# A new table of priority weights for the list scheduler of a top-k attention followed by two squared-ReLU feed-forward layers, one core

## The chip, the core and the metric

One core of a Trainium2 chip runs the whole program. Its engines work side by side, each through its own list of instructions in the order written: TensorE (PE, with its weight loads PEld), VectorE (DVE), ScalarE (ACT), GpSimd (POOL), and SyncE (SP), which here issues the DMAs. The metric is device microseconds of one execution; times are given as the median of the runs.

## What is computed

The reference, cut to its core (4 batches, 8 heads, 576 positions, head size 64, so 2304 tokens of 512; the hidden layers have 2048 columns):

```python
scores = scale * q @ k.T
kth = np.partition(scores, -32, axis=-1)[..., -32:-31]
scores = np.where(scores >= kth, scores, -1e9)          # keep the 32 largest of each row
attn = softmax(scores); x = (attn @ v), heads side by side
x = (s * relu(x @ w_in)**2 + b) @ w_out                 # first layer
x = relu(x @ w2_in)**2 @ w2_out                         # second layer
```

## The kernel before, in words

**Tiles.** 18 tiles of 128 queries (tiles 4 and 13 are made of two half tiles of two batches), 8 heads each: 144 heads of work. A head is: scores on PE (`pS`, L606, four matmuls), four rounds of MAX8 and three of MATCH_REPLACE on DVE to find the 32nd largest value (L617, L628), the exponential on ACT (`et`, L631), the mask on DVE (L659 or L665, which is the last reader of `pS`), a copy to two fp16 parts `pn` on ACT (L661, L668) and POOL (L463), a DMA transpose `pT` (L682), and 15 matmuls with the values on PE (`pA`, L692). Two score buffers `pS0` and `pS1` are used in turn, so the scores of a head wait for the mask of the head two before it.

**Two layers.** After its 8 heads a tile is scaled and split into fp16 parts: ACT squares it and sums (L704), DVE and POOL make a power of two of the sum, ACT scales (L708) and rounds (L710), POOL takes the rest (L711), and a DMA transpose makes `xT` (L713). A layer then runs over one tile or two ("a unit") in chunks of 256 hidden values: an IN group on PE (`pH`, L784, 12 matmuls of 256 columns or 24 of 128), on ACT `rr` (L792, ReLU, the only reader of `pH`), `gh` (L794, the square in fp16) and `gg` or `sqr` (L797, the square in fp32), on POOL `gl` (L802, the rest of the square), and an OUT group on PE (`pC`, L828, 6 matmuls of 512 columns). There are 288 chunks in all. `pH` is one buffer, `rr` two, `gh` and `gl` three.

**Weights.** The four weight matrices arrive as 64-bit words, are made to floats on DVE, ACT and POOL, scaled and split into fp16 parts (ACT L955, L956 and others), between the first heads.

**What sets the order.** Every operation is added to a `Plan` with an engine, a duration of its own, and a priority. `Plan.order` plays the program through with these durations and takes on each engine, at each moment, the ready operation of the lowest priority number; the resulting order is emitted as it is and not changed afterwards. To the priority it adds two numbers of a table `TW`: one under the name of the kind of work (the "tag", such as `A2.1` for tile 2, heads 2 and 3, `F08` for unit 8 of the first layer, `X2` for the split of tile 2), and one under the name of the step (such as `ac18` for `rr`).

Of the kernel before, what the change touches and what calls it, by code (L numbers as in the profile page):

```python
# [9 lines left out]
F16 = mybir.dt.float16  # L10
# [63 lines left out]


TW = {
# [41 lines left out]
}  # L118

WAIT = {("dve", "dve"): 0.2, ("act", "act"): 0.2, ("pool", "pool"): 0.1, ("pe", "pe"): 0.0, ("sp", "sp"): 0.0,  # L120
# [1073 lines left out]
```

## Time and profile before

| | |
|---|---|
| three runs | 1146.24, 1151.6 (median), 1153.46 us |
| the profiled execution | 1145.25 us, of which the span from the first to the last instruction is 1143.5 us |
| PE | 1014.8 us busy (89%) |
| DVE | 941.7 us (82%) |
| ACT | 844.6 us (74%) |
| POOL | 676.8 us (59%) |
| mean granted clock of PE | 0.964 |

A busy time is the time in which an engine has at least one instruction running. A share over the whole span is a mean over stretches that are limited by different things, so the rows below are cut by stretch. "Idle before <- X" is the time an engine sat idle just ahead of an instruction, and what ended it.

### The profile page before, as it was taken

What the parts mean: (1) busy time and instruction counts of PE and PEld (TensorE: products, weight loads), DVE (VectorE), ACT (ScalarE), POOL (GpSimd) and SP (SyncE); (2) the same over time, 40 slices, a digit from 0 to 9 for tenths busy, and PEclk for the clock granted to TensorE, in tenths of its full rate; (3) what the DMA queues carried; (4) which work ended last, traced back from release to release, by engine and by line L of the source; (5) the groups of instructions that cost most, each with busy time, mean ns of one, the idle gap of its engine ahead of it and who ended that gap; (6) DMA issues with size and microseconds to landing.
All of it is one profiled execution on the core that took longest, in us unless ns stands there. A gap on an engine that the chain in (4) does not pass through costs nothing. (4 is left out here: it accounts for less than half of the span.)

```text
span 1143.5 us, 27272 instructions
## 1 busy us (share of the span) xinstructions
PE 1014.8 (89%) x10004; PEld 690.7 (60%) x10004; DVE 941.7 (82%) x2038; ACT 844.6 (74%) x2010; POOL 676.8 (59%) x1005
## 2 busy tenths in 40 slices
PE   1256768777899999999999999999999999999998
PEld 1133335465667667667766776666666665666765
DVE  6999999899989999999999999997999999400000
ACT  2368987689788777889987889778876776565554
POOL 5267867889667655665865568456654464342322
PEclk9978889778999999999999999999999999999999
DMA  9988966584966776389486655776385257214530
GB/s 268 335 213 230 238 145 174 174 174 80 204 160 130 139 170 128 94 187 197 95 183 148 128 113 128 171 148 124 98 183 124 58 114 180 61 29 144 170 120 29
DMA packets 338215, 171.13 MB, mean 150 GB/s; under 512 B 292513, under 2 KB 317089, under 8 KB 338081
## 3 DMA queue, kind: packets, MB, share of 16 engines
q1 hardware_dynamic: 338080, 169.39, 63.0%
q8 instruction: 78, 1.28, 0.5%
q14 instruction: 57, 0.46, 0.1%
HBM read 89.65 MB, written 8.91 MB: 86 GB/s over the span
## 5 line engine op out<-in xcount | busy, mean ns | idle before, releaser
L784 PE MATMUL pH<-xT,w 128*128 128x128 f16 (+1 forms) x4800 | 431.6, 244 | 11.5 <-ACT rr L792 10.9
L784 PEld LDWEIGHTS <-w 128*128 128x128 f16 x4800 | 362.5, 98 | 75.4 <-issue 15.6
L463 POOL TENSOR_TENSOR pn<-et,pn 128x576 f16<-128x576 f32 x144 | 186.8, 1299 | 84.5 <-ACT pn L668 31.3
L792 ACT ACTIVATE rr<-pH,rsc 128x256 f32<-128x256 f32 x288 | 134.6, 467 | 96.6 <-PE pH L784 95.5
L802 POOL TENSOR_TENSOR gl<-gg,gh 128x256 f16<-128x256 f32 x152 | 102.9, 677 | 119.2 <-ACT gh L794 89.6
L828 PE MATMUL pC<-wo,gh 128*128 128x512 f16 x576 | 172.8, 382 | 0.0
L828 PE MATMUL pC<-wring,gh 128*128 128x512 f16 x544 | 161.9, 379 | 1.3 <-DMA wring<-wo 1.2
L617 DVE MAX8 m<-spare 128x8 f32<-128x576 f32 x216 | 161.8, 749 | 1.2
L617 DVE MAX8 m<-wk 128x8 f32<-128x576 f32 x216 | 161.5, 748 | 0.9
L828 PEld LDWEIGHTS <-gh 128*128 128x128 f16 x1152 | 103.4, 98 | 76.0 <-issue 3.0
L802 POOL TENSOR_TENSOR gl<-sqr,gh 128x256 f16<-128x256 f32 x136 | 91.3, 671 | 96.1 <-ACT gh L794 71.9
L631 ACT ACTIVATE et<-pS,ngm,cq 128x576 f32<-128x576 f32 x144 | 118.7, 826 | 27.4 <-DVE spare L628 11.2
L794 ACT ACTIVATE gh<-rr 128x256 f16<-128x256 f32 x288 | 118.3, 411 | 10.8 <-PE pC L828 4.3
L617 DVE MAX8 m<-pS 128x8 f32<-128x576 f32 x144 | 108.3, 754 | 12.2 <-PE pS L606 11.7
L692 PE MATMUL pA<-vp,pT 128*128 128x64 f16 (+1 forms) x2400 | 95.7, 197 | 17.5 <-DMA pT<-pn 17.3
L692 PEld LDWEIGHTS <-pT 128*128 128x128 f16 (+1 forms) x2400 | 86.9, 103 | 39.8 <-DMA pT<-pn 24.5
L828 PE MATMUL pC<-wo,gl 128*128 128x512 f16 x288 | 109.8, 381 | 0.0
L606 PE MATMUL pS<-kT,qT 128*128 128x512 f16 (+2 forms) x320 | 85.5, 298 | 24.1 <-DVE et L659 14.6
L628 DVE MATCH_REPLACE8 wk<-m,wk 128x576 f32<-128x576 f32 x144 | 106.8, 741 | 0.0
L628 DVE MATCH_REPLACE8 spare<-m,spare 128x576 f32<-128x576 f32 x144 | 106.7, 741 | 0.0
L828 PE MATMUL pC<-wring,gl 128*128 128x512 f16 x272 | 103.2, 379 | 0.6 <-POOL gl L802 0.6
L828 PEld LDWEIGHTS <-gl 128*128 128x128 f16 x576 | 56.4, 98 | 70.9 <-POOL gl L802 3.1
(197 smaller groups left out, 1627.8 us busy)
## 6 DMA issues: line engine op xcount, KB each, us to landing
wring<-wo SPq DMA_DIRECT2D x72, 512.0 KB, 3.8
w<-in_moe_w_out_dram SPq DMA_DIRECT2D x16, 512.0 KB, 5.0
wring<-in_moe_w_in_dram SPq DMA_DIRECT2D x12, 512.0 KB, 4.7
xT<-in_moe_w_in_dram SPq DMA_DIRECT2D x12, 512.0 KB, 5.3
qW<-qT SPq DMA_DIRECT2D x36, 128.0 KB, 2.7
kvraw<-in_k_dram SPq DMA_DIRECT2D x16, 256.0 KB, 3.4
kvraw<-in_v_dram SPq DMA_DIRECT2D x16, 256.0 KB, 3.1
w<-in_moe_w_in_dram SPq DMA_DIRECT2D x8, 512.0 KB, 7.8
```

Source lines behind the costliest of these rows:

```text
L463: add(pool, step, c_pool(cols * (c.stop - c.start) / n), prio, lambda c=c: nc.gpsimd.tensor_tensor(o[:, c], x[:, c], y[:, c], op=op), r=r, ...
L606: nc.tensor.matmul(s[r0:r0 + n, c0:c0 + cn_], lhsT=w[:, h, r0:r0 + n], rhs=kk[:, k0:k0 + cn_], start=(a == 0), stop=(a == 1))
L617: add(dve, "dv10", 0.67, prio, lambda src=src, rd=rd: nc.vector.max(m[:, 8 * rd:8 * rd + 8], src), r=[sn], w=[f"m{i2}_{rd}"])
L628: add(dve, "dv11", 0.66, prio, lambda src=src, rd=rd: nc.vector.match_replace(wk, m[:, 8 * rd:8 * rd + 8], src, NEG), r=[sn, f"m{i2}_{rd}" ...
L631: add(act, "ac9", 0.72, prio, lambda: nc.scalar.activation(out=e, in_=s, func=ACTF.Exp, bias=ngm[i2][:, 0:1], scale=cq[q2][:, j:j + 1]), r ...
L692: nc.tensor.matmul(pA[r0:r0 + n, h, :], lhsT=pT[p3][:, a * 5 + c, r0:r0 + n], rhs=vv[:, vc, z, :], start=(c == 0 and a == 0 and z == 0), s ...
L784: nc.tensor.matmul(ps_, lhsT=win[:, ff, a, kk, :], rhs=x[:, z * KD + kk, :], start=(kk == 0 and a == 0 and z == 0), stop=(kk == KD - 1 and ...
L792: add(act, "ac18", 0.14 + n / 1200.0, prio, lambda r=r, rs=rs: nc.scalar.activation(out=r, in_=pH[:, 0:n], func=ACTF.Relu, scale=rs), r=[" ...
L794: add(act, "ac19", 0.094 + n / 1200.0, prio, lambda r=r, hi=hi: nc.scalar.activation(out=hi, in_=r, func=ACTF.Square), r=rrn, w=ghn)
L802: add(pool, "po19", 0.12 + n * 0.0021, prio, lambda gt=gt, hi=hi, lo=lo: nc.gpsimd.tensor_tensor(lo, gt, hi, op=ALU.subtract), r=[*gn, *gh ...
L828: nc.tensor.matmul(pC[tt], lhsT=src[g3][:, c], rhs=wt(a, ff), start=(ff == 0 and a == 0 and src is gh), stop=(ff == KF - 1 and src is gl))
```

## The change

Only the numbers of the table `TW` are different; all of its lines are. Two of them, before and after:

```diff
-    "A0.0": 9.3, "A0.1": -14.6, "A0.2": 61.0, "A0.3": -2.7, "A1.0": -26.5, "A1.1": 51.0, "A1.2": -52.3, "A1.3": -7.5,
...
-    "sp7": -38.5, "sp8": -29.8, "sp9": -14.1, "store": 31.5,
+    "A0.0": -6.7, "A0.1": -39.6, "A0.2": 49.4, "A0.3": -5.2, "A1.0": -36.3, "A1.1": 48.0, "A1.2": -41.9, "A1.3": 22.4,
...
+    "sp8": 35.9, "sp9": 64.5, "store": 2.4,
```

No operation is added, removed or altered. The same instructions stand on the same engines, in an order that differs in many small places. Three of them follow.

**First place, ACT, while the last weights of the second layer are split and tile 3 is attended.** `xs0_91` and `xn0_93` hold tile 2, `w2_68` the weights, `pn0` and `et` are of the heads; the last row is `rr` of the second layer's second chunk. Before:

```order
L704 ACTIVATE junk_89,xss2_200<-xs0_91 128x512
L523 ACTIVATE kvraw1_87<-kvraw1_87,ksc_138 128x576
L851 ACTIVATE xs1_92<-pC0_189,usc1_151 128x512
L661 ACTIVATE pn0_102,sums1_128<-et0_100 128x576
L525 CAST vp5_85<-kvraw1_87 128x9x64
L708 ACTIVATE xs0_91<-xs0_91,xsc2_144 128x512
L624 ACTIVATE ngm1_126<-m8_1_122,ncq1_134 128x1
L710 CAST xn0_93<-xs0_91 128x512
L631 ACTIVATE et1_101<-pS1_186,ngm1_126,cq1_132 128x576
L955 ACTIVATE w2_68<-w2_68,wsc2_172 128x512 x2
L956 CAST w2_68<-w2_68 128x512 x2
L792 ACTIVATE rr0_111<-pH_188,rsc1_182 128x256
```

In the change, from the `et1_101` row on, on the same engine:

```order
L631 ACTIVATE et1_101<-pS1_186,ngm1_126,cq1_132 128x576
L523 ACTIVATE kvraw1_87<-kvraw1_87,ksc_138 128x576
L593 ACTIVATE ncq0_133<-cq0_131 128x1
L525 CAST vp5_85<-kvraw1_87 128x9x64
L955 ACTIVATE w2_68<-w2_68,wsc2_172 128x512 x2
L956 CAST w2_68<-w2_68 128x512 x2
L792 ACTIVATE rr0_111<-pH_188,rsc1_182 128x256
```

The three rows on tile 2 (L704, L708, L710) and the copy of `pn0` (L661) no longer stand ahead of this `rr`. The three rows now come four and five chunks later:

```order
L704 ACTIVATE junk_89,xss2_200<-xs0_91 128x512
L704 ACTIVATE junk_89,xss5_203<-xs1_92 128x512
L792 ACTIVATE rr0_111<-pH_188,rsc1_182 128x256
L624 ACTIVATE ngm0_125<-m8_0_121,ncq1_134 128x1
L797 ACTIVATE gg_113<-rr0_111 128x256
L661 ACTIVATE pn1_103,sums1_128<-et1_101 128x576
L631 ACTIVATE et0_100<-pS0_185,ngm0_125,cq1_132 128x576
L794 ACTIVATE gh2_116<-rr0_111 128x256
L708 ACTIVATE xs0_91<-xs0_91,xsc2_144 128x512
L624 ACTIVATE ngm1_126<-m8_1_122,ncq1_134 128x1
L710 CAST xn0_93<-xs0_91 128x512
L792 ACTIVATE rr1_112<-pH_188,rsc1_182 128x256
```

The rows of DVE, POOL and SP on tile 2 (L449, L451, L453, L711, L713) move back with them.

**Second place, PE, just after that chunk: what follows the scores of a head.** `pS1` is the score buffer, `pA` the product with the values, `pH` an IN group. Before:

```order
L606 LDWEIGHTS qT1_96
L606 MATMUL pS1_186<-kT2_76,qT1_96 128x64
L606 LDWEIGHTS qW1_98
L606 MATMUL pS1_186<-kT2_76,qW1_98 128x64
L692 LDWEIGHTS pT2_106
L692 MATMUL pA_187<-vp1_81,pT2_106 128x64
```

In the change:

```order
L606 LDWEIGHTS qT1_96
L606 MATMUL pS1_186<-kT2_76,qT1_96 128x64
L606 LDWEIGHTS qW1_98
L606 MATMUL pS1_186<-kT2_76,qW1_98 128x64
L784 LDWEIGHTS w2_68
L784 MATMUL pH_188<-xT2_109,w2_68 128x128
```

The `pA` group has gone behind two IN groups and an OUT group.

**Third place, ACT in the last stretch, the second layer of the last units.** Each chunk has its three rows. Before:

```order
L792 ACTIVATE rr0_111<-pH_188,rsc1_182 128x256
L797 ACTIVATE gg_113<-rr0_111 128x256
L794 ACTIVATE gh1_115<-rr0_111 128x256
L792 ACTIVATE rr1_112<-pH_188,rsc1_182 128x256
L797 ACTIVATE sqr_90<-rr1_112 128x256
L794 ACTIVATE gh2_116<-rr1_112 128x256
```

In the change:

```order
L792 ACTIVATE rr0_111<-pH_188,rsc1_182 128x256
L794 ACTIVATE gh1_115<-rr0_111 128x256
L797 ACTIVATE gg_113<-rr0_111 128x256
L792 ACTIVATE rr1_112<-pH_188,rsc1_182 128x256
L794 ACTIVATE gh2_116<-rr1_112 128x256
L797 ACTIVATE sqr_90<-rr1_112 128x256
```

`gh` now comes ahead of `gg`. On PE the same stretch reads IN, OUT, IN, OUT in both, but an OUT group belongs to the third IN group before it in the kernel before, and to the second in the change (at the very end four OUT groups follow the last IN group before, three in the change).

## Rows read from the trace of the kernel before

**Rows 1.** Busy time by stretch: us, each engine (instructions), PE clock, DMA share, GB/s.

```profile
0.00:300.00 300.00, 188.54 (x1650) 118.82 (x1651) 280.22 (x605) 216.47 (x469) 208.75 (x253) 0.86 0.78 202
300.00:985.00 685.00, 671.68 (x7090) 466.15 (x7087) 657.34 (x1421) 543.71 (x1346) 418.43 (x667) 1.00 0.65 140
985.00:1143.50 158.50, 154.61 (x1270) 105.75 (x1268) 4.17 (x14) 84.45 (x196) 49.61 (x86) 1.00 0.30 91
```

**Rows 2.** Chain of waits late in the span: start, us, an IN group, an OUT group.

```profile
1012.74 1.31 PE pH L784 x12
1014.05 1.29 PE pC L828 x6
```

**Rows 3.** Waits of PE from 300 us on: total us, times, longest.

```profile
PE pH L784 <- ACT rr L792: 4.4, 9, 0.9
PE pA L692 <- DMA pT<-pn: 3.5, 10, 0.7
PE pS L606 <- DVE et L665: 2.3, 4, 0.7
...
PE pC L828 <- POOL gl L802: 0.6, 2, 0.4
```

**Rows 4.** Busy time by stretch of 10 us, columns as in rows 1.

```profile
270.00:280.00 10.00, 3.19 (x38) 2.03 (x38) 10.00 (x27) 10.00 (x22) 9.82 (x20) 0.72 0.31 69
280.00:290.00 10.00, 8.68 (x104) 7.29 (x104) 8.80 (x18) 8.90 (x23) 9.31 (x10) 0.76 0.52 118
290.00:300.00 10.00, 8.55 (x124) 6.58 (x122) 9.75 (x21) 9.81 (x27) 7.60 (x13) 1.00 0.90 193
```

**Rows 5.** PE in order of time, 262 to 318 us: start, us, [idle before].

```profile
274.64 0.59 PE L606 MATMUL pS<-kT,qT 128*128 128x512 f16 x1 [2.74 <-DVE xsa L449]
...
278.12 0.98 PE L692 MATMUL pA<-vp,pT 128*128 128x64 f16 x15 [2.36 <-DMA pT<-pn]
280.70 2.72 PE L784 MATMUL pH<-xT,w 128*128 128x128 f16 x24 [1.60 <-ACT rr L792]
...
301.95 1.50 PE L784 MATMUL pH<-xT,w 128*128 128x128 f16 x24
```

**Rows 6.** ACT in order of time, 262 to 300 us: start, us.

```profile
272.80 0.62 ACT L704 ACTIVATE junk<-xs 128x512 bf16<-128x512 f32 x1
...
274.65 0.67 ACT L661 ACTIVATE pn<-et 128x576 f16<-128x576 f32 x1
...
275.88 0.72 ACT L708 ACTIVATE xs<-xs,xsc 128x512 f32<-128x512 f32 x1
...
276.68 0.61 ACT L710 CAST xn<-xs 128x512 f16<-128x512 f32 x1
...
280.17 0.47 ACT L792 ACTIVATE rr<-pH,rsc 128x256 f32<-128x256 f32 x1
```

**Rows 7.** DMA queue in order of time, 270 to 305 us: start, us of issue.

```profile
280.95 1.23 SPq L713 DMA_TRANSPOSE xT<-xn  x1
...
294.75 2.89 SPq L682 DMA_TRANSPOSE pT<-pn  x2
```

**Rows 8.** Issue to landing of these transposes, 270 to 310 us: min, median, max.

```profile
DMA to landing us min/median/max: 2.7/3.1/3.6
```

**Rows 9.** POOL in order of time, 275 to 303 us.

```profile
279.77 1.16 POOL L711 TENSOR_TENSOR xn<-xs,xn 128x512 f16<-128x512 f32 x1
...
296.68 0.19 POOL L867 TENSOR_TENSOR usc<-xsc,fc 128x1 f32<-128x1 f32 x1
```

**Rows 10.** DVE in order of time, 764 to 800 us.

```profile
776.41 0.15 DVE L449 TENSOR_SCALAR qsa<-qsc 128x1 int32<-128x1 int32 x1 [6.09 <-ACT junk L553]
...
778.86 0.77 DVE L617 MAX8 m<-pS 128x8 f32<-128x576 f32 x1 [2.11 <-PE pS L606]
```

**Rows 11.** ACT in order of time, 1000 to 1012 us.

```profile
1001.07 0.47 ACT L792 ACTIVATE rr<-pH,rsc 128x256 f32<-128x256 f32 x1 [1.11 <-PE pH L784]
```

**Rows 12.** POOL in order of time, 1000 to 1012 us.

```profile
1002.69 0.67 POOL L802 TENSOR_TENSOR gl<-gg,gh 128x256 f16<-128x256 f32 x1 [1.94 <-ACT gh L794]
```

78 rows, old and new, of the table TW are left out of this document.

## The prediction

> **What bounds the kernel now.** Nothing is added or taken away, so the question is only how long each engine sits idle, and whose idle time counts. I read the busy times by stretch first [rows 1]. Up to 300 us DVE works 280.22 of 300 us while PE works 188.54: the attention and the weights on DVE set the pace. From 300 to 985 us PE works 671.68 of 685 us and DVE 657.34, both over 95%. After 985 us DVE has nothing left, and PE works 154.61 of 158.50 us, the rest being the last result's way out. PE's time is therefore 111.5 us of idle ahead of 300 us, 13.3 us between, and 3.9 us at the end.
>
> Is PE really full after 300 us? The Trainium skill, "Perfetto Trace Analysis", Identifying the Most-Contended Engine, warns that matmul busy time is a poor measure and that the busy share of weight loads is to be taken. By that share PE would be 68% full here (466.15 of 685 us), and a better order could reach into the other 32%. The trace decides otherwise: an IN group of 12 matmuls of 256 columns takes 1.31 us and the OUT group of 6 matmuls of 512 columns follows at once and takes 1.29 us [rows 2]. That is 109 and 215 ns each, against 107 and 213 ns for as many columns at 2.4 GHz; nothing is left between them. So from 300 us on an order can give back 13.3 us at most, and more only by bringing PE to its dense stretch sooner.
>
> Next I read the waits of PE after 300 us [rows 3]: 4.4 us for `rr`, 3.5 us for `pT`, 2.3 us for the mask, 0.6 us for `gl`. These are small, many, and spread. Last I looked where the early stretch loses most just before PE becomes full. From 270 to 280 us PE works 3.19 of 10 us, and the granted clock is 0.72 there and 0.76 in the next 10 us; from 270 to 300 us PE sits idle 9.6 us. DVE, ACT and POOL are full in the worst of these (10.00, 10.00 and 9.82) [rows 4].
>
> **The change part by part.** I counted the two orders against each other on PE and DVE: for each of the 144 heads, what stands ahead of its scores on PE and ahead of its first maximum on DVE. Up to head 24 (about 265 us) the numbers of conversions, IN, OUT and `pA` groups are equal; later they differ by one to three groups. So the early 111.5 us stay, but for the places below. All terms are against the profiled execution, 1145.25 us.
>
> *First and second place, 265 to 290 us.* PE's IN group at 280.70 us waited for `rr`, which ACT reached only at 280.17 [rows 5, 6], because it stood behind other work in ACT's queue. In the change four instructions leave that queue ahead of it: L704, L661, L708 and L710, 0.62 + 0.67 + 0.72 + 0.61 = 2.6 us [rows 6]. `rr` could then run at about 277.5 us and PE's group at about 278. From there the gain is passed on only in part: the next scores on PE wait for a mask from DVE, which is full. The `pA` group that goes behind two IN groups and an OUT group did not wait where it stood, so its own move gives nothing; but the OUT group ahead of it may now wait for `gl`, with `pA` and the next scores queued behind. Lower bound of the saving nothing (DVE's full 10 us set the pace), upper bound 9.6 us of idle if all of 270 to 300 us closed. I take 2 us, near the 2.6 us that leave the queue.
>
> *What is late instead: tile 2.* Its rows go back on ACT, DVE, POOL and SP. Its POOL step stood at 279.77 us and now stands behind an instruction that ran at 296.68; its transpose, issued at 280.95, now follows two `pT` transposes issued from 294.75 to 297.64 [rows 7, 9]. I put it at 298.5 us, landed 2.7 to 3.6 us later [rows 8], so at about 302. The first IN group on tile 2 ran at 301.95 [rows 5]; in the change two pairs of scores and one more group stand ahead of it, some 3 us on PE. It fits with 3 us to spare: 0, with 3 us of loss as the other bound.
>
> *Heads 66 to 106, about 510 to 735 us.* Scores stand one or two groups (1.3 to 2.6 us) earlier on PE. They wait for the mask of the head two before. PE loses up to 2.6 us, but once: after that PE's work is shifted against DVE's and fits again. I take 1 us. From head 112 on they stand one to three groups later, and DVE waits instead; PE's remaining work is shorter by the same amount, which costs nothing.
>
> *The 8.2 us hole of DVE at 770 to 779 us* [rows 10]. The rows at this place, the query's scale between heads 109 and 110, and the DMA rows ahead of its load are the same in both. It stays, and PE works through it in both.
>
> *Third place, the shorter lead.* From chunk 150 on the change keeps an OUT group nearer to its IN group: the PE work between them (group lengths of rows 2, and 0.5 us for scores or `pA`) falls from 8.5 to 5.7 us in the mean of the last 88 chunks, and to 2.6 us in six chunks. Against that stands the time from the end of an IN group to the end of `gl`. At its fastest it is 2.3 us from the start of `rr` to the end of `gl` (1001.07 to 1003.36) [rows 11, 12], and 0.2 us more for the release. The reordering of `gh` ahead of `gg` comes from this: with a lead of two, its buffer is free when ACT comes to it. In the last stretch 5.2 us of lead cover 2.5 us. Before 985 us ACT and POOL also serve attention; an ACT or POOL instruction of 0.8 or 1.3 us in the way makes the six tight chunks wait some 0.2 us each. I take 1 us, lower bound nothing, upper bound 6 times 2.3 us, 14 us, if the chain took twice its shortest time each time.
>
> *All else* are exchanges inside queues where the instruction behind isn't waited for: 0, covered by the slack that leaves PE's waits at a dozen microseconds in 685.
>
> The sum: 1145.25 − 2 + 0 + 1 + 1 = 1145 us. The profiled execution is the fastest of the four times shown (1145.25, 1146.24, 1151.6, 1153.46); their mean is 1149. A median of new runs should fall near that, so I forecast 1149 us, no change that can be told: one per cent, 11.5 us, is about what a measurement of this kernel can tell.
>
> **The rivals.**
>
> *The hole at 270 us closes, and the clock with it (faster).* If PE is fed from 270 us on, it gains the 9.6 us of idle, and the clock stays at its upper level of 2.4 GHz: 0.72 and 0.76 mean 10.4 us at the lower level of 1.2 GHz [rows 4], 5.2 us of work. Together 15 us: 1134 us. For it speaks that the clock fell when PE worked 3 of 10 us. Against it, DVE was full there. The Trainium skill, "TensorE: Matmul & The Clock Gate", The HAM clock gate, says that the default is the throttled state and that activity lifts it; its terms put the penalty at throttled time times the missing share, which for a mean clock of 0.964 over 1143.5 us is an estimate of 41 us. By that rule such an order could gain 41 us; by the rows most of this lies under DVE's 280.22 us of work, and the trace agrees with the rule only in that the clock is full after 300 us.
>
> *The shorter lead starves PE (slower).* From chunk 150 to 985 us there are some 80 chunks. If ACT or POOL comes 0.2 us late for each, 16 us: 1165 us. It decides from 0.15 us a chunk on. Against it, PE waited only 0.6 us for `gl` after 300 us [rows 3], with the longer lead.
>
> *Tile 2 lands late (within 1%).* The 3 us bound above: 1152 us.
>
> **How the numbers follow.** The forecast has 0.55, tile 2 late 0.13, the closed hole 0.20, the starved PE 0.12. Faster by over 1% (under 1140) is the closed hole, 0.20; slower (over 1163) the starved PE, 0.12; the rest, 0.68, lies within. The range leaves out half of each outer case: 1135 to 1161 us. Its width is the bounds: 14 us down and 12 us up.
>
> **What would show it.** Right: PE busy from 300 us to the end of attention still at 97 to 99%, the start of the dense stretch within 3 us of 300, DVE's hole near 770 us still there, `rr` of the second layer's second chunk some 2 us sooner. A PE idle sum after 300 us over 25 us, with waits for `gl` or `rr`, would show the short lead; a wait of PE near 305 us for `xT`, tile 2. A clock of 1.00 from 270 to 290 us with PE over 8 of 10 us busy would show the first rival. The forecast is wrong if the time leaves 1140 to 1163 us.

## The result and the profile after

The changed kernel takes 1136.6 us in the mean of 10 executions (1134.2 to 1138.2), against 1149.6 us in the mean of 101 executions of the kernel before (1140.2 to 1156.8) that ran beside the experiments below. Left out here and below are the two executions that ran over 1.5% above the fastest of their kernel (1157.93 us of before, 1153.18 us of one experiment). In four executions each, taken side by side with the prediction, the ratio is 0.9882 with an interval of 0.9845 to 0.9919, so the kernel is faster by 1.2%, 13 us. The range of the prediction (1135 to 1161 us) holds 1136.9, the median of these four, 2 us from its lower end. The forecast, no change that can be told, was wrong, and by the sign that the prediction set itself (a time outside 1140 to 1163 us) it was wrong too.

The scatter changed as much as the time. The 113 executions with the order of before (101 and 12 of a repeat) fall in two heaps, 37 about 1145 us and 76 about 1152 us (parted at 1149). The 10 executions with the changed order stand in one heap, 4 us wide. The execution of before that the prediction was read from (1145.25 us) belongs to the lower heap.

Busy time by stretch of the changed kernel's profiled execution (1136.14 us, span 1134.4 us), columns as in [rows 1], which it answers:

```profile
0.00:300.00 300.00, 190.08 (x1732) 119.94 (x1733) 285.09 (x618) 219.93 (x479) 210.87 (x259) 0.89 0.81 204
300.00:985.00 685.00, 674.66 (x7077) 468.81 (x7076) 650.12 (x1410) 543.13 (x1345) 417.02 (x667) 1.00 0.66 140
985.00:1134.40 149.40, 145.48 (x1198) 99.68 (x1195) 3.42 (x11) 75.72 (x187) 45.94 (x80) 1.00 0.30 94
```

The attention is ahead when the dense stretch begins: 34 heads have had their first maximum by 300 us, and 32 before. PE works 1.5 us more up to 300 us (190.08 against 188.54) and 3.0 us more from there to 985 us (674.66 against 671.68), so it has 4.5 us less to do in the last stretch. Its busy time over the whole span is 4.6 us less too (1010.2 against 1014.8), as it had fewer microseconds at the lower clock (0.89 of full speed up to 300 us, 0.86 before). The last stretch is 9.1 us shorter by these two together. The waits of PE from 300 us on, with the same columns as [rows 3]:

```profile
PE pA L692 <- DMA pT<-pn: 3.3, 6, 0.8
PE pC L828 <- DMA wring<-wo: 2.5, 1, 2.5
PE pH L784 <- ACT rr L792: 2.2, 6, 0.5
PE pS L606 <- DVE et L665: 0.6, 2, 0.4
```

`rr` has fallen from 4.4 to 2.2 us, the mask from 2.3 to 0.6, and `gl`, 0.6 us before, has no row. The wait for `wring`, the ring that brings the second layer's output weights, is up from 1.2 us (two waits) to 2.5 us.

### The profile page after: what moved, and what is told of

The parts are those of the page before. It is cut to its first block, busy times and chain, and to the rows that moved or that the text cites. A ratio compares the mean times of both kernels' runs of the same rounds, so it can differ in the third digit from the quotient of the medians.

```text
span 1134.4 us, 27165 instructions
## 1 busy us (share of the span) xinstructions
PE 1010.2 (89%) x10004; PEld 688.4 (61%) x10004; DVE 938.6 (83%) x2038; ACT 838.8 (74%) x2010; POOL 673.8 (59%) x1005
## 4 chain that ended last, share of the span: by engine, by line
PE 33%; DVE 22%; DMA 3%; ACT 2%; issue 1%; DVEq 0%; ACTq 0%; SPq 0%
PE pH L784 15%; PE pC L828 15%; DVE m L617 10%; DVE wk L628 4%; DVE spare L628 4%; DMA pT<-pn 3%; PE pA L692 2%; PE pS L606 2%; DVE et L659 2%; DVE et L665 1%; ACT et L631 0%; ACT rr L792 0%; DVE xs L750 0%; ACT pn L661 0%; ACT pn L668 0%
```

## The experiments

All kernels compute the same thing with the same instructions. The orders of before and of the change have the same instructions behind them on every engine at certain places, the "clean cuts" (heads 9, 25, 46 and 108, at 120, 240, 370 and 730 us of the planner's time). At such a place one order can be joined to the other. The edit, with only PARTS different from kernel to kernel ("b" is the table of before, "a" the changed one):

```diff
-        prio += TW.get(self.tag, 0.0) + TW.get(step, 0.0)
+        self.prios.append({w: prio + t.get(self.tag, 0.0) + t.get(step, 0.0) for w, t in (("b", TW), ("a", TW_AFTER))})
...
-        for i in self.order():
+        for i in joined(self):
...
+PARTS = [('a', 370.0), ('b', 1000000000.0)]
+def joined(plan):
+    out, had = [], set()
+    for w, cut in PARTS:
+        part = [i for i in plan.order(w) if i not in had and plan.st[i] < cut]
+        had.update(part)
+        out += part
+    return out
```

Ratios are against executions of the kernel before on the same chip, with a 95% interval; microseconds behind a ratio are its distance from 1, times 1149 us. The chips differ (the mean of before is 1148.9, 1151.0, 1149.2 and 1149.5 us on the four used), so ratios are to be compared, and means only with that in mind. The theories: **A**, each stretch of the order makes its own part of the gain; **B** and **C**, all of it is late or early; and, as rivals on the early part, VectorE's stalls (**D**), the first two places of the prediction (**F**), and the clock.

### Where the gain lies

**The changed order up to head 46** (PARTS as above).

> The changed order up to the 47th head (about 390 us), the order of before behind it. The two traces put the gain of 9.1 us of span in two places: 3.7 us up to that head, where TensorE sat idle equally long (114.1 and 114.0 us) but had less time at its lower clock (81.9 us in all before, 68.3 after), and some 5 us behind it, 4.5 of them fewer idle us of TensorE. Theory A, both are made by the order of their own stretch: this kernel comes at 1149 - 4 = 1145 us, and if the wide scatter of the kernel before (1143 to 1153) is made by its early order too, at 1137 + 5 = 1142 us with a scatter of 2 us. Theory B, the early gain is chance of one execution (the clock falls at other moments in each), all that is lasting lies behind 390 us: 1149 us, scattered like before. Theory C, all lasting gain is early: 1137 us.

Mean 1141.2 us (1138.5 to 1146.1), ratio 0.9944 (0.9922 to 0.9966): 6.4 us.

**The changed order from head 46 on** (`PARTS = [('b', 370.0), ('a', ...)]`).

> The order of before up to the 47th head (about 390 us), the changed order behind it. Theory A (each stretch makes its own part): 1149 - 5 = 1144 us, still scattered over some 10 us; after 390 us TensorE idle near 10 us in place of 14.6. Theory B (all that lasts lies behind 390 us): 1137 to 1140 us. Theory C (all lasting gain is early): 1149 us.

Mean 1142.9 us (1136.1 to 1148.4), ratio 0.9956 (0.9926 to 0.9986): 5.1 us, still spread over 12 us. The two halves add up to 11.5 of the 13 us, which the intervals allow: theory A. The early order makes the scatter too.

**The kernel before once more** (a blank behind one number).

> The kernel before once more, for its scatter and for a second trace of it. If its scatter of 10 us comes from the clock in the first 300 us: the time lies within 1143 to 1154 us, the stretches at the lower clock lie elsewhere than in the first trace, and the time follows their sum (81.9 us gave 1145.25); behind head 46 the trace agrees with the first to 1 us. If the scatter comes from elsewhere: the early stretch agrees to 1 us and the later one differs.

Mean 1150.5 us, nine of twelve in the upper heap, and the profiled execution with them (span 1150.9 us). Its first maximum of head 22 stood 1.3 us ahead of the first trace's, that of head 25 5.2 us behind, and from head 51 on it stayed between 6.2 and 8.4 us behind. Part of what was expected fell: the heaps do not follow the time at the lower clock. The mean granted clock is 0.9695 in the upper heap and 0.9720 in the lower, which is 5.9 us more at the lower level of 1.2 GHz (twice the missing share of 1149 us), and over the 113 executions the time rises 0.17 us with each such us: one microsecond of the 7 between the heaps.

What happened at head 23, in order of time, first VectorE and then POOL, in this trace:

```profile
240.81 0.74 DVE L628 MATCH_REPLACE8 wk<-m,wk 128x576 f32<-128x576 f32 x1
241.47 4.55 DVE L937 SCALAR_TENSOR_TENSOR w<-wring,w 128x512 int32<-128x512 int32 x1
```

```profile
240.23 2.27 POOL L463 TENSOR_TENSOR w<-w 128x512 f16<-128x512 f32 x2
242.47 1.27 POOL L463 TENSOR_TENSOR pn<-et,pn 128x576 f16<-128x576 f32 x1
243.70 0.66 POOL L802 TENSOR_TENSOR gl<-gg,gh 128x256 f16<-128x256 f32 x1
244.33 1.14 POOL L711 TENSOR_TENSOR xn<-xs,xn 128x512 f16<-128x512 f32 x1
```

VectorE's conversion of a weight (L937) takes 4.55 us instead of 0.7. It ends 0.55 us after POOL has run two `w`, `pn`, `gl` and `xn` without a gap, and POOL's next instruction is 3.7 us away. That it is POOL that holds it can be read from all of its kind: up to 300 us this trace has 21 VectorE instructions drawn out by over 0.25 us, the first trace 17, all of them conversions of weights (L923, L930, L937), and every one ends 0.28 us (L923) or 0.55 us (the other two) after the end of a POOL instruction. The 576 maxima, the 432 replacements and the 144 masks of either trace differ by 0.07 us at most among their kind. In the first trace, the lower heap, the same instruction is not held:

```profile
242.78 0.74 DVE L937 SCALAR_TENSOR_TENSOR w<-wring,w 128x512 int32<-128x512 int32 x1
```

```profile
241.80 2.73 POOL L463 TENSOR_TENSOR w<-w 128x512 f16<-128x512 f32 x2
244.50 1.46 POOL L463 TENSOR_TENSOR pn<-et,pn 128x576 f16<-128x576 f32 x1
```

Here L937 comes 0.98 us after the start of the two `w`, of which the first takes 1.17, and runs between them. Above it came 1.24 us after, when the second had begun. All six traces with the order of before up to there fall this way: 0.97 to 0.98 us and 0.73 to 0.74 us of duration in four, 1.24 and 1.25 us with 4.55 and 4.54 us in two. A quarter of a microsecond decides over four.

Where it comes from stands two steps earlier, in POOL's `gl` ahead of the two `w` and in the IN group that its `gg` goes back to. First trace:

```profile
237.09 2.75 PE L784 MATMUL pH<-xT,w 128*128 128x128 f16 x24
241.18 0.67 POOL L802 TENSOR_TENSOR gl<-gg,gh 128x256 f16<-128x256 f32 x1 [0.24 <-ACT gg L797]
```

The long execution:

```profile
235.78 2.04 PE L784 MATMUL pH<-xT,w 128*128 128x128 f16 x24
239.60 0.66 POOL L802 TENSOR_TENSOR gl<-gg,gh 128x256 f16<-128x256 f32 x1
```

In all four traces with a short L937 this IN group takes 2.75 us, ACT's `rr` waits 0.45 to 0.46 us for it and `gl` 0.24 us for `gg`. In the two with a long L937 it takes 2.04 and 1.76 us, because the granted clock rises while it runs (1.50 us is its time at 2.4 GHz), and neither waits. So POOL comes to the two `w` earlier against VectorE when the clock rises sooner, and the execution gets longer by it. With the changed order the same group takes 1.96 to 2.72 us in seven traces, `rr` waits for it in each (0.38 to 1.89 us), and L937 takes 1.11 us at most. This is read from the traces; no experiment moved the clock alone.

Then the stall spreads, first on ACT, then on PE, in the long execution:

```profile
247.73 0.29 ACT L624 ACTIVATE ngm<-m,ncq 128x1 f32<-128x1 f32 x1 [5.48 <-DVE m L617]
247.93 0.46 ACT L792 ACTIVATE rr<-pH,rsc 128x256 f32<-128x256 f32 x1
```

```profile
248.43 2.72 PE L784 MATMUL pH<-xT,w 128*128 128x128 f16 x24 [4.81 <-ACT rr L792]
```

`ngm` waits 5.48 us for a maximum that stands behind L937 on VectorE, `rr` stands behind `ngm`, and PE's IN group waits 4.81 us for `rr`. The clock falls here as well (0.72 from 245 to 250 us, 1.00 in the 5 us before): the IN group takes 2.72 us, and 1.50 at 2.4 GHz. The fall comes after PE's stall has begun and is not its cause.

The Trainium skill, "SBUF — State Buffer", SBUF: two separate sides, says that VectorE and GpSimd share one pair of ports as an exclusive lock for whole instructions, for a VectorE instruction with two inputs in SBUF among others. The trace agrees in that L937 ends only behind POOL's run, and differs in how long: held to the end of the one POOL instruction under way it would take about 1.7 us, and it took 4.55, over four POOL instructions. Why POOL kept its turn at three boundaries is not shown by any run here.

**The changed order between heads 9 and 25** (`PARTS = [('b', 120.0), ('a', 240.0), ('b', ...)]`).

> The changed order only between head 9 (about 128 us) and head 25 (about 255 us), the order of before ahead of it and behind. In the two traces this stretch alone took 5.9 us less (heads 10 to 24: 0.9 us later became 4.7 us earlier). If the order of this stretch makes it, by keeping TensorE at its upper clock while scores wait behind it: 1149 - 5.8 = 1143 us, and the lower clock of 209.6 to 216.4 us, with VectorE idle 2.5 us behind it, is gone. If it is chance of one execution: 1149 us.

Mean 1148.4 us, ratio 0.9997 (0.9969 to 1.0026). It told nothing: behind the join at head 9 ACT waited 3.2 us for the load of a query, and VectorE stood idle 4.1 us between heads 9 and 15 where other traces show 0 to 2.3. One loss hid one gain.

**The changed order up to head 25** (`PARTS = [('a', 240.0), ('b', ...)]`).

> The changed order up to head 25 (about 255 us), the order of before behind it. Means of the first study: before 1148.9, changed order up to head 46 1141.2, changed order from head 46 on 1143.8 us. Theory D (VectorE sets the pace up to head 34, and the changed order lets it stand still or be held up less there: idle plus drawn-out instructions up to head 34 are 36.1, 42.1 and 33.8 us in three traces with the order of before, 32.1 and 31.7 us with the changed one, most of the difference ahead of head 25): 1141 to 1143 us, as with the change up to head 46. Theory F (the first two places of the prediction, heads 28 to 30, make it): 1147 to 1149 us. Theory C (the clock makes it): the mean follows the time at the lower clock, 0.2 us for each us less.

Mean 1144.8 us (1141.5 to 1147.4), ratio 0.9954 (0.9926 to 0.9982): 5.3 us, and one heap. Nearly all of the early gain lies ahead of head 25, as theory D says, though not as low as its 1141 to 1143.

**The changed order from head 25 to head 46** (`PARTS = [('b', 240.0), ('a', 370.0), ('b', ...)]`).

> The changed order from head 25 to head 46 (about 255 to 390 us) alone: the first two places of the prediction, and tile 2 behind them; the order of before elsewhere. The prediction's own terms for it: 2 us gained at heads 28 to 30, and nothing (at worst 3 us) lost where tile 2 arrives late, 1147 to 1150 us. In the traces the gain at heads 28 and 29 is 3.9 us (the hole of TensorE ahead of its IN group at 280.7 us), and 1.2 to 3.3 us are given back at heads 33 and 34. Theory D: 1148 us. Theory F: 1143 to 1145 us.

Mean 1148.3 us, ratio 0.9979 (0.995 to 1.0007): by its middle 2.4 us, but no gain at all lies within the interval as well. The traces say it more finely. VectorE's time from the first maximum of head 25 to that of head 30 (read from its rows in order of time) is 32.7 to 33.9 us in eight traces with the order of before, 30.5 to 31.1 in six with the changed one; from head 30 to head 34 it is 24.6 to 26.0 against 25.4 to 27.9. By the means 2.8 us are gained and 0.9 given back.

**The changed order from head 108 on** (`PARTS = [('b', 730.0), ('a', ...)]`).

> The changed order from head 108 on (about 757 us), the order of before ahead of it. The gaps of TensorE over 0.15 us between 830 and 990 us sum to 6.6, 6.9 and 8.1 us in three traces with the order of before, at the same heads with the same sizes (0.75 and 0.56 us in head 125, 0.69 us in head 133), and to 2.3 and 2.4 us with the changed one; between 390 and 850 us they sum to 3.4 to 5.0 us with both. If the late gain of 5 us lies in these gaps, 1148.9 - 4.5 = 1144.4 us, with the scatter of before. If it lies between heads 46 and 108, or was chance: 1148 to 1149 us. If the shorter lead of the third place cost anything, gaps ahead of OUT groups for the fp32 rest of POOL would be there: above 1149 us.

Mean 1147.3 us, ratio 0.9977 (0.9949 to 1.0006), 2.6 us by its middle, and here too the interval takes in 1; its profiled execution is another of the upper heap (L937 4.54 us at head 23). PE's idle time between heads 120 and 143 is 1.7 us in it, against 6.8 to 8.9 us in seven traces with the late order of before.

**The changed kernel once more.**

> The changed kernel once more, for its scatter and its clock. If its gain came from a better clock, its mean granted clock over the runs lies above that of before (0.9715 in 35 runs, some 66 us at the lower clock) by what pays for it. If it came from fewer stalls, the clock is the same within 0.002 and the time is 1137 us, scattered over 3 us in place of 15.

Mean 1136.3 us of six (1134.2 to 1138.1), ratio 0.9882 (0.9838 to 0.9927). Over all ten the mean granted clock is 0.9718, against 0.9703 in the 113 executions of before: 3.4 us less at the lower level, worth 0.6 us by the slope above. Time at the lower clock is not where 13 us come from. In the first traces of before and of the change the lower level held for 81.9 and 68.3 us. It looked like the cause, and was worth 2.3 us of that pair's 9.1 by the same slope.

### Two rows of POOL

Two causes remained to be taken alone. The first edit moves two instructions of POOL at head 23, as the change does, and nothing else on any engine:

```diff
-        for i in self.order():
+        for i in moved(self.order()):
...
+MOVES = [(953, 835), (744, 1125)]
+def moved(out):
+    for i, j in MOVES:
+        out.remove(i)
+        out.insert(out.index(j), i)
+    return out
```

> The kernel before with two rows of POOL alone moved, as they stand in the change: L711 (xn) goes from behind pn1 to ahead of a weight's L463, and one L463 of a weight goes behind pn1 and its gl (head 23, about 238 to 247 us); all other engines have the order of before. Five traces with the order of before in heads 20 to 25 take 41.3, 42.4, 42.6, 48.5 and 48.7 us for them; in the two long ones VectorE's L937 on a weight takes 4.55 us in place of 0.7, until POOL has run w, pn, gl and xn without a gap. With the changed order five traces take 40.6 to 42.2 us. Theory D2 (this pile-up makes the two heaps of times of before, near 1143 and near 1152 us, and is the early half of the gain): the mean falls by 5 us to 1144 to 1146 us, the upper heap is gone (none, or one in twelve, above 1149). Theory E (the pile-up is a symptom of something earlier, the clock for instance): two heaps and a mean near 1150 us as before.

Mean 1147.4 us (1144.6 to 1150.4), ratio 0.9981 (0.9958 to 1.0003). The heaps are gone and the spread is halved (2.0 us of standard deviation in place of 3.9), so the pile-up does make the heaps. The mean fell by only 2.2 us by the middle of an interval that takes in 1, not by 5: now L937 is held a little in the profiled execution, to the end of one `w`.

```profile
239.65 1.75 DVE L937 SCALAR_TENSOR_TENSOR w<-wring,w 128x512 int32<-128x512 int32 x1
```

```profile
239.06 0.67 POOL L802 TENSOR_TENSOR gl<-gg,gh 128x256 f16<-128x256 f32 x1
239.69 1.16 POOL L463 TENSOR_TENSOR w<-w 128x512 f16<-128x512 f32 x1
240.87 1.67 POOL L463 TENSOR_TENSOR pn<-et,pn 128x576 f16<-128x576 f32 x1
```

VectorE's time for heads 20 to 25 is 44.4 us in it. It is 41.3 to 43.1 us in the lower heap of before, 48.5 and 48.7 in the upper, and 40.6 to 42.2 us in seven traces with the changed order (that of the next experiment among them). If each execution of the upper heap has the pile-up of these two traces, 76 of 113 give before 46.5 in the mean, an estimate: 2.1 us more than this kernel's one trace (measured 2.2) and 5.1 more than the changed order (measured up to head 25: 5.3). That one trace has the early rise of the clock (its IN group takes 1.74 us and `rr` does not wait), the case that gave the long L937 before.

The converse, the two rows put back in the changed kernel (the same edit with `MOVES = [(953, 1125), (744, 1337)]`):

> The changed kernel with the same two rows of POOL put back to where they stand before, all else as changed. Theory D2: the pile-up can come back: two heaps, near 1137 and near 1145 us, mean 1139 to 1143 us, and scatter of over 6 us in place of 4; where the profiled execution is of the upper heap its L937 at head 23 takes some 4.5 us. Theory E: 1136.5 us, scattered over 4 us as the changed kernel.

Mean 1137.6 us of six, ratio 0.9894 (0.9863 to 0.9925), one heap. Theory D2 missed: the pile-up does not come back. The profiled execution says what else keeps it away:

```profile
237.09 0.68 POOL L802 TENSOR_TENSOR gl<-gg,gh 128x256 f16<-128x256 f32 x1 [1.25 <-ACT gg L797]
237.72 4.03 POOL L463 TENSOR_TENSOR w<-w 128x512 f16<-128x512 f32 x3
```

POOL waits 1.25 us for ACT's `gg` ahead of the `w`, three of them in a row now, and L937 (238.72, 0.71 us) comes 1.0 us after their start, inside the first. In the changed kernel this wait is 0.44 us. So the two rows of POOL alone are one sufficient way to be rid of the heaps and not the only one. That the change keeps POOL from running ahead of VectorE through the order on ACT is read from these waits; which rows of ACT do it was not tried.

### The lead of IN over OUT

One weight of the table of before changed, that of ACT's `gh`:

```diff
-    "ac14": 56.4, "ac15": 62.7, "ac16": 57.2, "ac17": 69.7, "ac18": -68.0, "ac19": -46.9, "ac2": 3.8, "ac20": 15.8,
+    "ac14": 56.4, "ac15": 62.7, "ac16": 57.2, "ac17": 69.7, "ac18": -68.0, "ac19": -37.2, "ac2": 3.8, "ac20": 15.8,
```

> The kernel before with one weight of the table as in the neighbourhood of the change (the square in fp16, from -46.9 to -37.2). The orders are the same up to head 108 (about 757 us) but for a few rows of ACT; behind it gh stands later than gg's neighbour and OUT groups keep closer to their IN groups in the last 140 chunks, the lead falling from 3.5 and 3.8 IN groups to 3.1 and 3.0 as in the change (2.8 and 2.9). If the shorter lead is what takes the late gaps of TensorE away: gaps between 830 and 990 us fall from 7 to under 4 us and the time by 3 to 4 us, to 1146 us with the two heaps of before. If the lead is neither good nor bad: 1150 us and gaps of 6 to 7 us, in other heads. If a shorter lead starves TensorE: above 1153 us, with gaps ahead of OUT groups that wait for the fp32 rest on POOL.

Mean 1146.4 us (1138.7 to 1152.7, two heaps as before), ratio 0.9974 (0.9942 to 1.0006): 3.0 us by its middle, with 1 still in the interval. PE's idle time between heads 120 and 143 is 3.5 us in its trace, so by the idle time one weight brings most of the late gain.

The other way round, one weight of the changed table put back:

```diff
-    "F11": 68.3, "F12": 0.2, "F13": -51.2, "F14": 46.3, "F15": -10.0, "F16": 9.3, "F17": 26.1, "F18": 2.3,
+    "F11": 68.3, "F12": 0.2, "F13": -51.2, "F14": -53.8, "F15": -10.0, "F16": 9.3, "F17": 26.1, "F18": 2.3,
```

> The changed kernel with one weight put back (F14, the IN groups of one later unit of the first layer, from 46.3 to -53.8). The order is the changed one up to head 100 (about 700 us); behind it OUT groups follow their IN groups at a distance again: the lead is 4.5 to 5 IN groups in the last 70 chunks where the change has 3 and the kernel before 4. If the short lead is what takes the gaps of TensorE away (idle of heads 120 to 143: 6.8 to 8.9 us in seven traces with the late order of before, 1.7 to 2.8 us in five with the changed one, 3.5 us where one weight of ACT alone shortened the lead): idle of 5 us or more there, and 1140 to 1142 us. If the gaps go away for other reasons (the exact places of scores among the groups): either value, without regard to the lead; 1137 us with idle under 3.5 us would say that the lead is neither good nor bad.

Mean 1141.3 us (1138.5 to 1143.4), ratio 0.993 (0.9904 to 0.9956): 4.7 us slower than the changed kernel in the mean, though on another chip (the intervals of the two ratios just overlap), and 6.1 us of idle PE between heads 120 and 143. The waits of PE between 830 and 985 us (total us, times, longest): before, the change, and the change with the long lead.

```profile
PE pS L606 <- DVE et L665: 2.3, 4, 0.7
PE pH L784 <- ACT rr L792: 1.9, 3, 0.7
PE pA L692 <- DMA pT<-pn: 1.1, 3, 0.5
PE pC L828 <- DMA wring<-wo: 0.7, 1, 0.7
PE pC L828 <- POOL gl L802: 0.6, 2, 0.4
```

```profile
PE pA L692 <- DMA pT<-pn: 1.3, 2, 0.8
PE pH L784 <- ACT rr L792: 0.7, 2, 0.4
PE pS L606 <- DVE et L665: 0.4, 1, 0.4
```

```profile
PE pS L606 <- DVE et L665: 2.6, 3, 1.4
PE pA L692 <- DMA pT<-pn: 2.0, 1, 2.0
PE pH L784 <- ACT rr L792: 0.9, 2, 0.7
PE pH L784 <- DMA xT<-xn: 0.4, 1, 0.4
```

The short lead costs no wait for `gl` at all (0.6 us before, none after). The long one comes with waits for the mask, 2.3 and 2.6 us against 0.4. Both edits moved attention too, so the lead is shown to go with the gaps, twice, in both directions, and not to be their cause; that IN groups which run far ahead use up PE time that scores would need later is my reading of it, and only argued.

## Why the prediction was wrong, and where it was right

**The forecast's time.** Its sum was 0 against 1145.25 us, moved to 1149 by "a median of new runs should fall near that". The scatter was taken for noise that the changed kernel would share. It belonged to the order, which another order of the same instructions does not have: an estimated 5.1 of the 13 us are the upper heap and some held-up instructions at heads 20 to 25. That the range holds the time is luck: its lower end was placed to take in half of the rival of the closed hole, and the hole did not close. Against the trace from which the sum was made the change gained 9.1 us (1145.25 to 1136.14), which is the sum's own error.

**"The early 111.5 us stay, but for the places below."** This step failed first. It counted what stands ahead of each head's scores and maxima, and those counts are equal up to head 24. What differs is the order of ACT and POOL between the same two heads, and on POOL it was not counted at all. VectorE's 280.22 busy us of [rows 1] were read as work. In that trace the 17 drawn-out VectorE instructions took 12.7 us more than the median of their kind, 0.28 to 1.09 us each, so an engine shown busy could still be given time.

**First and second place, 2 us.** Right in mechanism, and near in size: 2.8 us at heads 25 to 30. ACT and PE there, in the changed kernel:

```profile
273.00 0.46 ACT L792 ACTIVATE rr<-pH,rsc 128x256 f32<-128x256 f32 x1
```

```profile
273.51 2.42 PE L784 MATMUL pH<-xT,w 128*128 128x128 f16 x24 [0.18 <-ACT rr L792]
```

The IN group that waited 1.60 us [rows 5] waits 0.18 us; its `rr` runs 7.2 us earlier, where the chunk before it was only 3.9 us earlier: 3.3 us nearer, of which 2.6 us were the four instructions named.

**Tile 2, 0 us with 3 as the bound.** The cost was 0.9 us in the mean, 2.9 in the first trace, and it came by a road that was not named. Not `xT` but the ring load is late:

```profile
302.60 0.86 PE L828 MATMUL pC<-wring,gh 128*128 128x512 f16 x2 [2.55 <-DMA wring<-wo]
```

```profile
293.43 3.68 SPq L713 DMA_TRANSPOSE xT<-xn  x2
297.20 1.00 SPq L424 DMA_DIRECT2D wring<-wo  x2
```

The transpose of tile 2, moved back on SP's queue, and that of tile 1 between its two layers hold it for 3.68 us ahead of the ring's load. PE's waits for `wring` between 292 and 325 us are 2.8 to 3.7 us in six traces with this order, and 0.3 to 0.8 us in eight with the order of before.

**Heads 66 to 106, 1 us lost.** Not seen: PE's idle time from head 66 to 106 is 1.0 to 2.4 us with the order of before and 0.7 to 1.4 with the changed one.

**DVE's hole at 770 us.** Right, it stays: 7.58 us ahead of `qsa` where [rows 10] had 6.09.

```profile
771.94 0.15 DVE L449 TENSOR_SCALAR qsa<-qsc 128x1 int32<-128x1 int32 x1 [7.58 <-ACT junk L553]
```

**The shorter lead, 1 us lost, 14 as the bound.** Wrong in sign, as far as the lead makes the late gain. The step asked only whether OUT would wait for `gl` and took 1 us for it; no such wait came. It never asked what the longer lead had cost: from head 46 on PE sits idle 10.5 to 12.5 us with the order of before and 6.2 to 7.9 us with the changed one, 4.5 us in the mean. The waits for the mask and `rr` were in [rows 3], 6.7 us of them, and were put down as "small, many, and spread". In trace after trace they stand at the same heads with the same sizes (0.75 and 0.56 us in head 125, 0.69 us in head 133), which is the mark of an order and not of chance.

**The rivals.** The first gave the right side for the wrong reason. The hole shrank only a little (PE idles 10.3 to 12.1 us from head 25 to head 34, and 12.1 to 13.1 us with the order of before), and the clock fell there all the same, in the windows of 260 to 280 us:

```profile
260.00:270.00 10.00, 6.13 (x62) 3.57 (x60) 10.00 (x30) 9.79 (x19) 9.14 (x16) 0.93 0.33 47
270.00:280.00 10.00, 6.44 (x73) 5.32 (x73) 9.93 (x21) 10.00 (x25) 9.82 (x14) 0.73 0.33 81
```

The 15 us worked out from the clock are not what was gained, and the estimate of 41 us by the clock gate's rule (the Trainium skill, "TensorE: Matmul & The Clock Gate", The HAM clock gate) was not touched by this change: the mean clock went from 0.9703 to 0.9718. The second rival, starved PE, did not occur.

**What adds up.** Heads 20 to 25 5.1 us, heads 25 to 34 1.9, PE's idle time from head 46 on 4.5: 11.5 of 13.0 us. The remaining 1.5 us are within the intervals; they are not at heads 0 to 20 or 34 to 46, which take the same time in both orders to 0.3 us in the means.

## What to carry to other kernels

Before runs that scatter are taken for noise, profile a second execution of the same kernel and find the first instruction at which the two part; if they part at one place, an order can remove it. Read the duration of an engine's instructions against others of their kind and not its busy share alone, because a held-up instruction counts as busy. And where a change shortens a distance, price both ends: what the shorter one may cost, and what the longer one is costing now, wait by wait, in [rows 3].

## What the runs showed of the hardware

A VectorE instruction with two inputs in SBUF was held for 4.55 us while POOL ran four instructions without a gap, and came through at once (0.74 us) when it arrived 0.26 us sooner. What followed from it sets two executions of one program some 7 us apart. Time at the lower granted clock explains 1 us of these 7; yet in six traces of six it was the moment at which the clock rose, within one IN group (1.76 and 2.04 us) or after it (2.75 us), that went with the collision or its absence.

VectorE's drawn-out conversions of weights, 38 in two traces, all ended 0.28 or 0.55 us after the end of a POOL instruction.
